# The x of token groups 4 and 5 transposed on TensorE instead of by a DMA transpose

## The chip, the core and the metric

The kernel runs on one core of a Trainium2 chip (trn2). The metric is the device time of one execution in microseconds (us); the kernel before takes 300.17 us, the median of three executions (300.12, 300.17 and 301.02 us). A profiled execution gives the span from the first to the last instruction, 298.4 us, which is a little shorter than the execution's time.

In what follows PE is TensorE (PEld is its loading of weights), DVE is VectorE, ACT is ScalarE, POOL is GpSimd, and SP is SyncE, which computes nothing and here issues nearly all loads and all DMA transposes. A DMA transpose reads a tile from the on-chip memory and writes it back to the on-chip memory transposed, without any compute engine.

## What is computed

Chunked attention, followed by a feed-forward layer with a squared ReLU:

```python
# q, k, v: [8 batches, 8 heads, 576 tokens, 64]; float32
# tokens attend only within their own chunk of 64
scores = (1 / sqrt(64)) * q_c @ k_c.T            # per batch, head and chunk
attn   = softmax(scores)
x      = attn @ v_c                              # then heads side by side:
x      = x.transpose(0, 2, 1, 3).reshape(4608, 512)
h      = maximum(x @ w_in, 0)                    # w_in  [512, 2048]
out    = (h * h) @ w_out                         # w_out [2048, 512]
```

The kernel computes in bfloat16 with float32 sums.

## The kernel before

The 4608 tokens are cut into 18 groups of 256 tokens. Two groups make a block of 512 tokens; there are nine blocks, numbered j = 0 to 8: groups 0 and 1, groups 3 and 2, groups 4 and 5, 6 and 7, and so on. For each block the program runs the first matmul layer (`ffn_in`), then the second (`ffn_out`). The attention of later groups is placed in small steps between these matmuls, at numbered slots: a slot is one `yield` of `ffn_in` or `ffn_out`.

A group goes through these steps: its q and k are cast to bfloat16 (C) and transposed by DMA (TD), or, for the early groups, transposed on TensorE (TA); then scores and exp (SC); then the product with the values and the division (AV), which leaves `x`, tokens on partitions; then `x` is transposed (XT) to `xT`, features on partitions, since `ffn_in` needs it that way.

```python
    blocks = [[0, 1], [3, 2]] + [[g, g + 1] for g in range(4, n_grp, 2)]
    FIRST_DMA_T = 6          # from this group on, q and k are transposed by DMA
    FIRST_DMA_X = 4          # from this group on, x is transposed by DMA
    # ...
    def cast_qk(g):                                               # C, on GpSimd
        qkb = att_pool.tile([128, 2, 2 * H * D], BF16, name="qkb", bufs=2)
        # ... two casts, q and k
    def transpose_qk_dma(g):                                      # TD, issued by SP
        qkT = att_pool.tile([128, 2, 2, n_hp, 128], BF16, name="qkT", bufs=4)
        nc.sync.dma_start_transpose(
            out=qkT.rearrange("c w t h q -> c (w t h) q"),
            in_=qkb.rearrange("p w c -> p (w c)"))
    # ...
    def transpose_x(g):                                           # XT
        j, c = place[g]
        if j not in xTs:
            xTs[j] = att_pool.tile([128, BT // 128, n_dt, 128], BF16, name="xT", bufs=2)
        x = state.pop(("x", g))
        dst = xTs[j][:, c // 128:c // 128 + 2].rearrange("p t h q -> p (t h) q")
        if g >= FIRST_DMA_X:
            nc.sync.dma_start_transpose(out=dst, in_=x.rearrange("p t h a d -> p (t h a d)"))
            return
        ps = ps_att.tile([128, 1024], FP32, name="ps_att")
        psb = ps.bitcast(BF16)[:, 0:1024].rearrange("p (b q) -> p b q", q=128)
        for t in range(2):
            for hp in range(n_hp):
                nc.tensor.transpose(                              # 8 of 128x128, line 337
                    out=psb[:, t * n_hp + hp, :],
                    in_=x[:, t, hp].rearrange("p a d -> p (a d)"),
                    identity=ident)
        copy = nc.scalar.copy if g == 2 else nc.vector.tensor_copy
        copy(out=dst, in_=psb)                                    # line 342
```

The change acts in the plan of block j = 1. That block runs `ffn_in` in 32 slots (0 to 31, four matmuls of 256 columns each) and `ffn_out` in 16 slots (32 to 47, four matmuls of 512 columns each). Its matmuls have groups 3 and 2 for input; between them it prepares the next block (`nxt`: groups 4 and 5) and starts on the one after that (`far`: groups 6 and 7):

```python
        elif j == 1:
            loads = itertools.chain(*map(qk_pieces, far), v_pieces(far[0]))
            go_slots = range(14, 32)          # one load is issued at each of these slots
            # ... group 2: TA, SC, AV, XT at slots 1, 5, 8, 12
            for i, g in enumerate(nxt):       # groups 4 and 5
                for slot, f in ((21 + 4 * i, TA), (28 + 2 * i, SC), (33 + 2 * i, AV),
                                (36 + 2 * i, XT)):
                    at(slot, f, g)
            for i, g in enumerate(far):       # groups 6 and 7
                at(34 + 3 * i, C, g)
                at(39 + 3 * i, TD, g)
```

In block j = 2 the scores of groups 6 and 7 come at slots 8 and 11, their values at 12 and 16, and the transposes of their x at 16 and 19. An `ffn_in` slot there is four matmuls of 512 columns.

Line numbers in the profile that matter here: 123, 130 and 145 are loads (q and k, values of the even heads, values of the odd heads), 272 the DMA transpose of q and k, 286 the scores, 310 the product with the values, 318 the division that writes `x`, 331 the DMA transpose of `x`, 337 and 342 the TensorE transpose of `x` and its copy out of PSUM, 355 the matmuls of `ffn_in`, 402 those of `ffn_out`, and 422 those of the first block's `ffn_out`.

Of the kernel before, what the change touches and what calls it, by code (L numbers as in the profile page):

```python
# [17 lines left out]
def kernel(  # L18
# [21 lines left out]

    blocks = [[0, 1], [3, 2]] + [[g, g + 1] for g in range(4, n_grp, 2)]
    FIRST_DMA_T = 6
    FIRST_DMA_X = 4
    BT = GT * max(len(b) for b in blocks)

    const_pool = ctx.enter_context(tc.tile_pool(name="const", bufs=1))
# [80 lines left out]
    def v_pieces(g):  # L127

        for t, p, m, b, s in runs(g):
            yield lambda t=t, p=p, m=m, b=b, s=s: nc.sync.dma_start(  # L130
                out=v_even[g % NV][p:p + m, t, :, 0:D],
                in_=v[b, 0::2, s:s + m, :].rearrange("h s d -> s h d"))

        g0, g1 = GT * g, GT * (g + 1)
        for n in range(2 * g, 2 * g + 3):
            lo, hi = max(0, 128 * n - 64), min(n_tokens, 128 * n + 64)
            if g in (1, 2, 3):
                lo, hi = max(lo, 320 if g == 1 else g0), min(hi, g1)
            elif g > 3:
                lo = max(lo, g0 if g == 4 else g0 + 64)  # L140
            if lo >= hi:
                continue
            p = lo - (128 * n - 64)
            for b, s, m in segments(lo, hi - lo):
                yield lambda n=n, p=p, m=m, b=b, s=s: nc.sync.dma_start(  # L145
                    out=v_odd[n % NO][p:p + m, :, 0:D],
                    in_=v[b, 1::2, s:s + m, :].rearrange("h s d -> s h d"))
                p += m

    def go(pieces):  # L150
        for f in pieces:
            f()
# [171 lines left out]
    def transpose_x(g):  # L324
# [4 lines left out]
# [3 lines that stand above are left out]
# [12 lines left out]
    C, TD = cast_qk, transpose_qk_dma  # L344
    SC, AV, XT = scores, values, transpose_x
# [24 lines left out]
    def ffn_in(j, parts):  # L370
        for c, n, ft in ((c, n, ft) for c, n, fts in parts for ft in fts):

            o, per = ft * n % 512, 512 // n
            if o == 0:
                h = ps_ffn.tile([128, 512], FP32, name="ps_ffn")
            mm_in(j, h, o, ft, c, n)
            if o + n == 512:
                relu2(j, h, ft + 1 - per, per, c)
            yield

    def ffn_out(j):
        gT = gTs.pop(j)
        n_tt = len(blocks[j]) * GT // 128
        for tt in range(n_tt):
            if j == len(blocks) - 1 and tt == n_tt - 1:

                t0 = blocks[j][tt // 2] * GT + tt % 2 * 128
                for dma, c in ((nc.scalar, 0), (nc.sync, 256)):
                    o_ps = ps_ffn.tile([128, d_model], FP32, name="ps_ffn")
                    for ft in range(n_ft):  # L390
                        nc.tensor.matmul(  # L391
                            out=o_ps[:, 0:256],
                            lhsT=gT[:, ft, tt * 128:(tt + 1) * 128],
                            rhs=w_out_bf[:, ft, c:c + 256],
                            start=(ft == 0), stop=(ft == n_ft - 1))
                    o_sb = ffn_pool.tile([128, d_model], FP32, name="o_sb", bufs=4)
                    nc.vector.tensor_copy(out=o_sb[:, 0:256], in_=o_ps[:, 0:256])
                    dma.dma_start(out=out[t0:t0 + 128, c:c + 256], in_=o_sb[:, 0:256])
                continue
            o_ps = ps_ffn.tile([128, d_model], FP32, name="ps_ffn")  # L400
            for ft in range(n_ft):
                nc.tensor.matmul(  # L402
                    out=o_ps,
                    lhsT=gT[:, ft, tt * 128:(tt + 1) * 128],
                    rhs=w_out_bf[:, ft, :],
                    start=(ft == 0), stop=(ft == n_ft - 1))
                if ft == n_ft - 1:
                    t0 = blocks[j][tt // 2] * GT + tt % 2 * 128
                    o_sb = ffn_pool.tile([128, d_model], FP32, name="o_sb", bufs=4)
                    nc.scalar.copy(out=o_sb, in_=o_ps)  # L410
                    nc.gpsimd.dma_start(out=out[t0:t0 + 128, :], in_=o_sb)  # L411
                if ft % 4 == 3:
                    yield

    def ffn_out_by_ft(j):

        gT = gTs.pop(j)
        n_tt = len(blocks[j]) * GT // 128
        o_ps = [ps_ffn.tile([128, d_model], FP32, name="ps_ffn") for _ in range(n_tt)]

        def mm(tt, ft):
            nc.tensor.matmul(  # L422
                out=o_ps[tt],
                lhsT=gT[:, ft, tt * 128:(tt + 1) * 128],
                rhs=w_out_bf[:, ft, :],
                start=(ft == 0), stop=(ft == n_ft - 1))

        for ft in range(n_ft - 4):
            for tt in range(n_tt):
                mm(tt, ft)  # L430
            yield
        for tt in range(n_tt):
            for ft in range(n_ft - 4, n_ft):
                mm(tt, ft)
            o_sb = ffn_pool.tile([128, d_model], FP32, name="o_sb", bufs=4)
            nc.scalar.copy(out=o_sb, in_=o_ps[tt])
            t0 = blocks[j][tt // 2] * GT + tt % 2 * 128
            nc.gpsimd.dma_start(out=out[t0:t0 + 128, :], in_=o_sb)
            yield

    def pieces(grps):
        for g in grps:
            yield from qk_pieces(g)
        for g in grps:
            yield from v_pieces(g)
# [44 lines left out]
    for j, grps in enumerate(blocks):  # L490
        nxt = blocks[j + 1] if j + 1 < len(blocks) else []
        far = blocks[j + 2] if j + 2 < len(blocks) else []
        plan = {}

        def at(slot, f, g):
            plan.setdefault(slot, []).append((f, g))

        if j == 0:
            loads, go_slots = pieces(far), range(17)
            for slot, f in ((22, TA), (25, SC), (26, AV), (28, XT)):  # L500
                at(slot, f, nxt[0])
            phases = [ffn_in(0, [(0, 512, range(2, n_ft))]), ffn_out_by_ft(0)]
        elif j == 1:
            loads = itertools.chain(*map(qk_pieces, far), v_pieces(far[0]))
            go_slots = range(14, 32)
            for slot, f in ((1, TA), (5, SC), (8, AV), (12, XT)):
                at(slot, f, grps[1])
            for i, g in enumerate(nxt):
                for slot, f in ((21 + 4 * i, TA), (28 + 2 * i, SC), (33 + 2 * i, AV),
                                (36 + 2 * i, XT)):  # L510
                    at(slot, f, g)
            for i, g in enumerate(far):
                at(34 + 3 * i, C, g)
                at(39 + 3 * i, TD, g)
            phases = [ffn_in(1, [(0, 256, range(n_ft)), (256, 256, range(n_ft))]), ffn_out(1)]
        else:
            loads, go_slots = pieces(far), range(32)
            slots = {SC: 9 if j == 3 else 8, AV: 11, XT: 15, C: 14, TD: 19}
            if j == 2:
                loads = itertools.chain(v_pieces(nxt[1]), loads)  # L520
                go_slots = [*range(14), 17, 18, *range(22, 32)]
                slots = {SC: 8, AV: 12, XT: 16, C: 16, TD: 21}
            for i, g in enumerate(nxt):
                at(slots[SC] + (3 * i if j == 2 else 0), SC, g)
                at(slots[AV] + 4 * i, AV, g)
                at(slots[XT] + 3 * i, XT, g)
            for i, g in enumerate(far):
                at(slots[C] + 2 * i, C, g)
                at(slots[TD] + 3 * i, TD, g)
            phases = [ffn_in(j, [(0, BT, range(n_ft))]), ffn_out(j)]  # L530
        slot = 0
        for phase in phases:
            for _ in phase:
                if slot in go_slots:
                    for f in loads:
                        f()
                        break
                for f, g in plan.get(slot, []):
                    f(g)
                slot += 1  # L540
        go(loads)
# [30 lines left out]
```

## Time and profile before

| | |
|---|---|
| time, median of 3 | 300.17 us |
| span of the profiled execution | 298.4 us |
| PE busy | 285.6 us, 96% of the span |
| ACT, DVE, POOL busy | 131.3, 108.2, 65.4 us |
| DMA transposes of x (line 331) | 14, landing 3.0 to 6.2 us after issue, median 3.3 |
| DMA transposes of q and k (line 272) | 12, landing 5.2 to 8.9 us after issue, median 5.7 |
| TensorE transposes of x at line 337 | 16 (groups 3 and 2) |

The profile's page gives busy times, the span in 40 slices with the granted clock of TensorE, the chain of work that ended last, and groups of instructions. For each group it says how long one instruction takes and how long its engine stood idle before it, and for what. Idle time on an engine other than the one that sets the end costs nothing by itself. The timeline shows instructions in order of time; for the queue of SP an entry is the issue of a DMA, not its landing. Where a matmul row gives a mean of 359 to 383 ns, this is the time of one from start to end; matmuls overlap in the pipeline, so the spacing of a row of them is read from the starts in the chain or in the timeline.

### The profile page before, as it was taken

How to read it: one execution, taken by the hardware profiler on the slowest of the kernel's cores; microseconds unless marked ns; L12 is line 12 of the kernel's file. 1: busy time of each engine (PE TensorE's matmuls, PEld its weight loads, DVE VectorE, ACT ScalarE, POOL GpSimd, SP SyncE). 2: the span in 40 equal slices, each digit the busy share in tenths (PEclk: the TensorE clock that was granted, in tenths of full speed). 3: DMA queues.
4: the chain of work that ended last, by engine and by line, in shares of the span. 5: the costliest groups of instructions: out<-in, count | busy, mean ns of one | idle time of the engine just before them, and what ended most of it. 6: DMA issues, size and time to landing. Idle time of an engine off the chain costs nothing.

```text
span 298.4 us, 6449 instructions
## 1 busy us (share of the span) xinstructions
PE 285.6 (96%) x2645; PEld 141.0 (47%) x2645; DVE 108.2 (36%) x232; ACT 131.3 (44%) x214; POOL 65.4 (22%) x103
## 2 busy tenths in 40 slices
PE   6899998999949999999999999999999999999995
PEld 3454445885414444444444444444444444444444
DVE  0467314564103450356037405630662046205401
ACT  1556224775105731672167217712671177126510
POOL 2067634000430241033105014201420100020010
PEclk9999999999997999999999999999999999999999
DMA  7999999997999999999999999699967501310011
GB/s 235 247 348 368 346 268 246 237 206 169 231 232 193 222 182 233 221 213 172 231 227 218 182 265 236 122 175 271 253 120 153 161 36 21 86 73 35 0 73 70
DMA packets 147933, 56.52 MB, mean 189 GB/s; under 512 B 129024, under 2 KB 143616, under 8 KB 147904
## 3 DMA queue, kind: packets, MB, share of 16 engines
q1 hardware_dynamic: 144960, 46.81, 77.1%
q0 software_dynamic: 2800, 9.18, 9.0%
q8 instruction: 21, 0.34, 0.5%
q10 hardware_dynamic: 144, 0.13, 0.1%
q14 instruction: 8, 0.07, 0.1%
HBM read 36.70 MB, written 9.44 MB: 155 GB/s over the span
## 4 chain that ended last, share of the span: by engine, by line
PE 79%; DMA 10%; SPq 7%; POOL 2%; issue 1%; DVE 0%; DVEq 0%
PE ps_ffn L355 38%; PE ps_ffn L402 33%; DMA w_st<-in_moe_w_out_dram 5%; DMA w_st<-in_moe_w_in_dram 4%; SPq L130 3%; PE ps_att L310 2%; SPq L145 2%; DMA xT<-x 2%; PE ps_att L286 2%; SPq L123 1%; PE ps_ffn L391 1%; PE ps_ffn L422 1%; PE ps_att L191 1%; POOL w_out_bf L174 1%; POOL w_in_bf L167 1%
## 5 line engine op out<-in xcount | busy, mean ns | idle before, releaser
L355 PE MATMUL ps_ffn<-xT,w_in_bf 128*128 128x512 bf16 (+3 forms) x648 | 131.5, 359 | 4.0 <-DMA xT<-x 4.0
L367 DVE TENSOR_TENSOR gT<-rl 128x512 bf16<-128x512 bf16 x144 | 69.9, 496 | 147.3 <-ACT rl L365 145.9
L402 PE MATMUL ps_ffn<-w_out_bf,gT 128*128 128x512 bf16 x496 | 108.9, 379 | 0.0
L365 ACT ACTIVATE rl<-ps_ffn 128x512 bf16<-128x512 f32 x144 | 85.1, 599 | 42.4 <-PE ps_ffn L355 41.0
L355 PEld LDWEIGHTS <-w_in_bf 128*128 128x128 bf16 x648 | 61.6, 98 | 65.2 <-issue 6.6
L402 PEld LDWEIGHTS <-gT 128*128 128x128 bf16 x496 | 47.9, 98 | 56.8
L410 ACT COPY o_sb<-ps_ffn 128x512 f32<-128x512 f32 x31 | 18.2, 586 | 92.3 <-PE ps_ffn L402 92.3
L411 POOL DMA_DIRECT2D out_dram<-o_sb x31 | 16.8, 541 | 124.2 <-ACT o_sb L410 124.2
L265 POOL CAST qkb<-qk_sb 128x1024 bf16<-128x1024 f32 x24 | 26.7, 1125 | 74.1 <-DMA qk_sb<-in_q_dram 72.2
L318 DVE TENSOR_TENSOR x<-ps_att,rec 128x512 bf16<-128x512 f32 x36 | 24.9, 691 | 1.2
L293 ACT ACTIVATE e<-ps_att 128x1024 bf16<-128x1024 f32 x18 | 17.7, 1023 | 2.3 <-PE ps_att L286 2.3
L422 PE MATMUL ps_ffn<-w_out_bf,gT 128*128 128x512 bf16 x64 | 15.0, 379 | 1.4 <-POOL w_out_bf L174 1.3
L174 POOL CAST w_out_bf<-w_st 128x1024 bf16<-128x1024 f32 x8 | 8.7, 1086 | 8.2 <-DMA w_st<-in_moe_w_out_dram 7.9
L259 PE MATMUL ps_ffn<-zeros 128*128 128x512 bf16 x29 | 8.9, 439 | 1.3 <-POOL zeros L58 1.3
L317 DVE RECIPROCAL rec<-ps_att 128x8 f32<-128x8 f32 x36 | 7.2, 199 | 8.2 <-PE ps_att L310 8.1
L310 PEld LDWEIGHTS <-e 64*64 64x64 bf16 x576 | 6.5, 107 | 7.5 <-issue 3.2
L422 PEld LDWEIGHTS <-gT 128*128 128x128 bf16 x64 | 6.0, 98 | 8.5 <-issue 1.6
L310 PE MATMUL ps_att<-ve_sb,e 64*64 64x65 bf16 x288 | 8.8, 196 | 0.1
L310 PE MATMUL ps_att<-vo_sb,e 64*64 64x65 bf16 x288 | 8.7, 196 | 0.0
L200 ACT COPY qkT<-ps_att 128x512 bf16<-128x512 bf16 x8 | 4.3, 589 | 9.9 <-PE ps_att L191 9.9
L167 POOL CAST w_in_bf<-w_st 128x1024 bf16<-128x1024 f32 x7 | 7.6, 1086 | 2.9 <-DMA w_st<-in_moe_w_in_dram 2.9
L286 PEld LDWEIGHTS <-qkT 64*64 64x64 bf16 x576 | 5.7, 108 | 4.7 <-issue 3.0
(34 smaller groups left out, 58.5 us busy)
## 6 DMA issues: line engine op xcount, KB each, us to landing
out_dram<-o_sb POOLq DMA_DIRECT2D x35, 256.0 KB, 4.2
qk_sb<-in_q_dram SPq DMA_DIRECT2D x23, 256.0 KB, 5.5
qk_sb<-in_k_dram SPq DMA_DIRECT2D x23, 256.0 KB, 5.6
ve_sb<-in_v_dram SPq DMA_DIRECT2D x32, 128.0 KB, 4.4
w_st<-in_moe_w_in_dram SPq DMA_DIRECT2D x8, 512.0 KB, 6.6
w_st<-in_moe_w_out_dram SPq DMA_DIRECT2D x8, 512.0 KB, 6.5
vo_sb<-in_v_dram SPq DMA_DIRECT2D x29, 128.0 KB, 3.8
qk_sb<-in_q_dram SPq DMA_DIRECT2D x1, 1024.0 KB, 5.7
```

What stands on the lines that cost most here:

```text
L174: nc.gpsimd.tensor_copy(out=w_out_bf[:, 2 * i:2 * i + 2, :], in_=st)
L265: nc.gpsimd.tensor_copy(out=qkb[:, which], in_=qk[g][which].rearrange("p t h d -> p (t h d)"))
L293: nc.scalar.activation(out=e.rearrange("p a h t q -> p (a h t q)"), in_=ps, func=AF.Exp, scale=scale)
L310: nc.tensor.matmul(out=ps[64 * p:64 * p + 64, a, hp * (D + 1):(hp + 1) * (D + 1)], lhsT=e[64 * c:64 * c + 64, a, hp, t, :], rhs=vb[64 * c: ...
L318: nc.vector.tensor_tensor(out=x[:, t].rearrange("p h a d -> p a h d"), in0=o[:, :, :, 0:D], in1=rec.to_broadcast([128, 2, n_hp, D]), op=AL ...
L355: nc.tensor.matmul(out=h[:, o:o + n], lhsT=w_in_bf[:, dt, ft * 128:(ft + 1) * 128], rhs=xT[:, c // 128:(c + n) // 128, dt, :], start=(dt = ...
L365: nc.scalar.activation(out=rl, in_=h, func=AF.Relu)
L367: nc.vector.tensor_tensor(out=gTs[j][:, ft:ft + per, c:c + 512 // per], in0=r3, in1=r3, op=ALU.mult)
L402: nc.tensor.matmul(out=o_ps, lhsT=gT[:, ft, tt * 128:(tt + 1) * 128], rhs=w_out_bf[:, ft, :], start=(ft == 0), stop=(ft == n_ft - 1))
L410: nc.scalar.copy(out=o_sb, in_=o_ps)
L411: nc.gpsimd.dma_start(out=out[t0:t0 + 128, :], in_=o_sb)
L422: nc.tensor.matmul(out=o_ps[tt], lhsT=gT[:, ft, tt * 128:(tt + 1) * 128], rhs=w_out_bf[:, ft, :], start=(ft == 0), stop=(ft == n_ft - 1))
```

## The change

The x of groups 4 and 5 is no longer transposed by two DMA transposes. It takes the way that groups 2 and 3 already take: eight TensorE transposes per group into PSUM, and one copy to `xT`, which is on VectorE for groups 4 and 5. The transposes are placed at slots 38 and 41 instead of 36 and 38. The DMA transposes of q and k of groups 6 and 7 move up three slots, from 39 and 42 to 36 and 39. The change is meant to spare the next block's first matmul the wait for a transfer, and SP's queue two entries.

```diff
-    FIRST_DMA_X = 4
+    FIRST_DMA_X = 6
...
                 for slot, f in ((21 + 4 * i, TA), (28 + 2 * i, SC), (33 + 2 * i, AV),
-                                (36 + 2 * i, XT)):
+                                (38 + 3 * i, XT)):
                     at(slot, f, g)
             for i, g in enumerate(far):
                 at(34 + 3 * i, C, g)
-                at(39 + 3 * i, TD, g)
+                at(36 + 3 * i, TD, g)
```

On the engines this adds 16 transposes to PE (eight after the 28th of the 64 matmuls of block 1's `ffn_out`, eight after the 40th) and two copies to DVE, and takes two DMA transposes from SP's queue. ACT and POOL have the same instructions in the same order.

## The prediction

> **What bounds the kernel now.** I read four views, in this order. First the page's totals and slices: TensorE is busy 96% of the span, so the other engines set the end only where TensorE waits for them.
>
> ```profile
> PE 285.6 (96%) x2645; PEld 141.0 (47%) x2645; DVE 108.2 (36%) x232; ACT 131.3 (44%) x214; POOL 65.4 (22%) x103
> ...
> PEclk9999999999997999999999999999999999999999
> ```
>
> The clock row has one dent, a 7 in the thirteenth slice. A slice is 298.4 / 40 = 7.46 us, so the dent lies between 89.5 and 97.0 us. Next, the groups: among the many matmuls of the two layers only line 355 has a wait worth naming.
>
> ```profile
> L355 PE MATMUL ps_ffn<-xT,w_in_bf 128*128 128x512 bf16 (+3 forms) x648 | 131.5, 359 | 4.0 <-DMA xT<-x 4.0
> L402 PE MATMUL ps_ffn<-w_out_bf,gT 128*128 128x512 bf16 x496 | 108.9, 379 | 0.0
> ```
>
> The end of the first row says that TensorE stood idle for 4.0 us, and that a DMA writing xT ended it. The table of waits says once, not 14 times. So one of the transposes of x comes late, and the others are hidden. The chain in order of time shows which one; the columns are start, length, what:
>
> ```profile
> 73.85 0.59 PE ps_att L310 x32
> 74.44 0.26 SPq L123
> ...
> 81.94 1.34 SPq L331
> ...
> 83.39 5.17 DMA xT<-x
> 88.56 0.14 issue
> 88.69 9.62 PE ps_ffn L355 x36
> 98.31 0.38 PE ps_att L286 x32
> ```
>
> It is the transpose of group 5, at the start of block 2. At 74.44 us the chain leaves TensorE for SP's queue. The timeline says why: x of groups 4 and 5 was written by 73.73 and 75.95 us, but SP issues in order, and before the two transposes it still had loads to issue, without a pause, until 81.83 us. The transposes went out at 81.94 and 83.39 us, the second took 5.17 us to land, and TensorE had run out of ffn_out's matmuls: 48 of them from 74.17 us at 217.5 ns (the spacing in block 2, 13.92 us for 64) end at 84.61 us.
>
> Last, the stretches. Columns: stretch, length, busy time of PE, PEld, DVE, ACT and POOL, granted clock, DMA share, GB/s.
>
> ```profile
> 84.70:88.70 4.00, 0.01 (x2) 0.04 (x2) 0.00 (x0) 0.59 (x1) 0.54 (x1) 1.00 1.12 275
> ...
> 89.50:92.90 3.40, 3.40 (x10) 1.22 (x8) 0.85 (x2) 1.20 (x2) 0.00 (x0) 0.50 1.43 169
> 92.90:98.30 5.40, 5.40 (x31) 2.31 (x33) 2.31 (x6) 3.58 (x6) 0.00 (x0) 1.00 0.96 214
> ```
>
> TensorE is idle for 4.0 us, and soon after it resumes its clock is halved for 3.4 us. "Busy 3.40" hides this: ten matmuls began there, where 3.40 / 0.216 = 15.7 would fit. The wait is thus paid for twice. The same stretch of the next block, also 36 matmuls between the start and the first scores, needs 7.77 us instead of 9.62:
>
> ```profile
> 149.68 7.77 PE ps_ffn L355 x36
> ```
>
> **What the Trainium skill says.** "TensorE: Matmul & The Clock Gate", section "Why this matters for your kernels", advises no idle gaps of TensorE over about 3 us, since the clock then falls to half; Part 1 there gives the activity window as 3413 ns and says that it runs freely. The trace agrees: 4.0 us idle, then 3.4 us at 0.50. Part 4 of the same page says that a TensorE transpose needs a copy out of PSUM afterwards, and that transposes don't count as activity in the same way; here eight last 0.45 to 0.60 us, and no dent follows those at 48 and 58 us. "VectorE: DVE Perf Modes", section "The three transpose paths", gives 390 ns for a TensorE transpose of 128x128 and 1309 ns for a DMA one. I use neither: in a row the trace spaces TensorE's far closer, and this DMA's cost is its place in the queue.
>
> **The change, part by part.**
>
> 1. *Removed: the wait.* TensorE would go on at 84.61 instead of 88.69 us: 4.08 us gained, all on the path.
> 2. *Removed: the half clock.* Without the pause I expect no throttle: 9.62 - 7.77 = 1.85 us gained, also on the path.
> 3. *Added on TensorE: 16 transposes.* The same instruction runs for groups 3 and 2 already:
>
> ```profile
> 48.40 0.45 PE ps_att L337 x8
> ...
> 57.80 0.60 PE ps_att L337 x8
> ```
>
> Two groups cost 2 x 0.45 = 0.90 to 2 x 0.60 = 1.20 us. They lie between matmuls of ffn_out and TensorE has no slack there, so all of it counts. I take the middle, 1.05 us.
> 4. *Added on VectorE: two copies of 128x1024.* One takes 0.69 us (line 342, group 3). From the last division at 75.95 us to 90.44 us VectorE does nothing, so both are hidden. Are they in time? Group 4's transposes start after 28 matmuls of ffn_out, at 74.17 + 12 x 0.2175 = 76.8 us, when both x are complete. Group 5's start 12 matmuls later, at 79.8 us; with the copy, xT is there by about 81.3 us. ffn_out now ends at 84.61 + 1.05 = 85.7 us, so over 4 us are left. The PSUM tiles of ps_att were last read by the division at 75.95 us and are free.
> 5. *Removed from SP: two issues, 2.8 us in all.* The transposes of q and k of groups 6 and 7 then follow the loads directly, at about 81.9 instead of 84.9 us. Nothing waits for them now (before, they land at 93.8 and 95.4 us; the scores start at 98.24 and 101.31), so no gain. But the question is whether they still land in time.
>
> Sum: 4.08 + 1.85 - 1.05 = **4.9 us**, from 300.17 to **295.3 us**, 1.6%.
>
> **Rivals.**
>
> *A: the next transposes become the wait.* TensorE reaches the scores of group 6 at 85.7 + 7.8 = 93.5 us, and those of group 7 after 12 more matmuls and the first scores, at about 96.5 us: each some 4.8 us sooner, while SP moves by only some 3 us. The first transpose, issued at 81.94 us, lands by 90.8 us even with the slowest landing on record (8.9 us): 2.7 us to spare. The second is issued after it, at 86.8 us if the first holds the queue for 4.8 us again, and lands at 92.3 us with 5.5 us, or 95.7 with 8.9: 0.8 us to spare at worst. Against the rival: the slow landing stood behind the two transposes that now go away. If it comes true, the gain falls by a microsecond or so, unless the pause grows long enough to halve the clock again.
>
> *B: SP's backlog shows a block later.* The last transpose of x for block 4 lands at 146.25 us and is needed at 149.68, a margin of 3.4 us. If TensorE moves by 4.9 us and SP by 2.8, the margin shrinks by 2.1 to 1.3 us. The transposes for block 3 land at 113.19 us for a start at 120.31: more room. From 188 us on SP pauses for x by itself, so the backlog is gone. I expect no wait, but one of up to 1 us is possible.
>
> *C: the transfer was hidden anyway, and the transposes only cost time:* about 301.2 us. This would be so had TensorE another reason to stand still at 84.6 us. Against it: the chain passes through this transfer, and other blocks start without a pause after their ffn_out. I give it almost nothing.
>
> *D: the wait goes, the half clock stays* (because transposes don't count as activity): 297.2 us. Against it: transposes fill only about 1 us of the 85.7 us before, and equal rows of them at 48 and 58 us left no dent.
>
> **Range and chances.** The sum with the cheapest transposes gives 295.1 us, with the dearest 295.4. I expect no reward in later blocks, since after 88.69 us TensorE has no pause that could shrink; the most that can be gained is 4.08 + 1.85 = 5.9 us, to 294.2, if the transposes cost nothing. On the slow side A and B can return a microsecond or so, and D 1.85. The medians wander by some tenths (one execution of three was 0.85 us above the others). So 295.3, range 294.6 to 296.9. A gain of over 2% needs a time below 294.17, beyond that largest gain: chance 0.03. Slower by over 2% would need a new pause of over 10 us: 0.01.
>
> **What would show it right or wrong.** Right: no wait of line 355 for xT; no dent in the clock row between 89 and 97 us; line 337 with 32 transposes, a row of eight taking 0.45 to 0.60 us; 36 matmuls in 7.8 us from about 85.7 us; then the same lengths as before in every later block. Step 3 is wrong if the two rows cost other than 0.9 to 1.2 us, seen as ffn_out of block 1 growing by another amount. Rival A would show as a wait of line 286 for qkT near 93 or 96 us, B as a wait of line 355 for xT near 145 us, D as a halved clock with no pause ahead of it.

## The result, and the profile after

The changed kernel takes **295.63 us** (median of four executions, 295.15 to 296.68) against 300.14 us before on the same chip: a ratio of 0.985, with a 95% interval of 0.9815 to 0.9886. The gain is 4.5 us; 4.9 was predicted.

From the page of the changed kernel, the same rows as those shown of before: totals, clock in 40 slices, the two layers' matmuls.

```profile
PE 285.2 (97%) x2661; PEld 141.7 (48%) x2661; DVE 111.1 (38%) x234; ACT 131.2 (45%) x214; POOL 64.7 (22%) x103
...
PEclk9999999999999999999999999999999999999999
...
L355 PE MATMUL ps_ffn<-xT,w_in_bf 128*128 128x512 bf16 (+3 forms) x648 | 129.8, 356 | 0.0
...
L402 PE MATMUL ps_ffn<-w_out_bf,gT 128*128 128x512 bf16 x496 | 109.3, 379 | 0.0
```

The wait of 4.0 us at the end of the row of line 355 is 0.0, and the dent in the clock is gone. The 16 added transposes show only in the counts (2645 to 2661): "busy" of TensorE is even 0.4 us lower, since matmuls at half clock count as busy for longer (line 355 falls from 131.5 to 129.8 us), and the idle time had never counted. The chain that ended last, around the end of block 1 (start, length, what):

```profile
74.87 2.70 PE ps_ffn L402 x12
77.57 0.45 PE ps_att L337 x8
78.02 2.59 PE ps_ffn L402 x12
80.61 0.45 PE ps_att L337 x8
81.05 5.18 PE ps_ffn L402 x24
86.23 7.77 PE ps_ffn L355 x36
94.00 0.38 PE ps_att L286 x32
```

The chain stays on TensorE. Before, it left for SP's queue at 74.44 us and came back at 88.69. The two rows of transposes take 0.45 us each, block 2 starts at once after ffn_out, and its first 36 matmuls take 7.77 us instead of 9.62.

In the span (298.4 to 294.1 us) the gain is 4.3 us. The balance: block 1's ffn_out starts 0.64 us later than before (70.53 against 69.89 us). In this execution TensorE stood still for 0.88 us at 55.6 us, inside line 310, and the profile names no releaser for it. From there to block 3 (69.89 to 120.31 us before, 70.53 to 116.01 after) the gain is 4.94 us.

### The profile page after: what moved, and what is told of

It reads as the page before. It is cut to its first block, busy times and chain, and to the rows that moved or that the text cites. A ratio compares the mean times of both kernels' runs of the same rounds, so it can differ in the third digit from the quotient of the medians.

```text
span 294.1 us, 6475 instructions
## 1 busy us (share of the span) xinstructions
PE 285.2 (97%) x2661; PEld 141.7 (48%) x2661; DVE 111.1 (38%) x234; ACT 131.2 (45%) x214; POOL 64.7 (22%) x103
## 4 chain that ended last, share of the span: by engine, by line
PE 83%; DMA 9%; SPq 4%; POOL 2%; issue 1%; DVE 0%; DVEq 0%
PE ps_ffn L355 38%; PE ps_ffn L402 37%; DMA w_st<-in_moe_w_out_dram 5%; DMA w_st<-in_moe_w_in_dram 4%; PE ps_att L310 2%; SPq L130 2%; PE ps_att L286 2%; SPq L145 2%; PE ps_ffn L391 1%; PE ps_ffn L422 1%; PE ps_att L191 1%; POOL w_out_bf L174 1%; POOL w_in_bf L167 1%; PE ps_att L337 1%; POOL w_in_bf L163 1%
## 5 line engine op out<-in xcount | busy, mean ns | idle before, releaser
L355 PE MATMUL ps_ffn<-xT,w_in_bf 128*128 128x512 bf16 (+3 forms) x648 | 129.8, 356 | 0.0
L367 DVE TENSOR_TENSOR gT<-rl 128x512 bf16<-128x512 bf16 x144 | 71.3, 508 | 136.3 <-ACT rl L365 135.0
L265 POOL CAST qkb<-qk_sb 128x1024 bf16<-128x1024 f32 x24 | 26.0, 1105 | 69.0 <-DMA qk_sb<-in_q_dram 67.8
L259 PE MATMUL ps_ffn<-zeros 128*128 128x512 bf16 x29 | 9.5, 464 | 1.3 <-POOL zeros L58 1.3
```

Source lines behind the costliest of these rows:

```text
L265: nc.gpsimd.tensor_copy(out=qkb[:, which], in_=qk[g][which].rearrange("p t h d -> p (t h d)"))
L355: nc.tensor.matmul(out=h[:, o:o + n], lhsT=w_in_bf[:, dt, ft * 128:(ft + 1) * 128], rhs=xT[:, c // 128:(c + n) // 128, dt, :], start=(dt = ...
L367: nc.vector.tensor_tensor(out=gTs[j][:, ft:ft + per, c:c + 512 // per], in0=r3, in1=r3, op=ALU.mult)
```

## The experiments

**1. The moves without TensorE.** The changed plan, x still by DMA:

```diff
-    FIRST_DMA_X = 6
+    FIRST_DMA_X = 4
```

> The changed plan with the transposes of x of groups 4 and 5 left to the DMA: on SP's queue they now come in the order q and k of 6, x of 4, q and k of 7, x of 5. Theory (the gain is the wait for xT taken away; the moves bring nothing by themselves): x of group 5 is issued some 6 us later than in the kernel before, at about 88 to 90 us, lands at about 93 us, the pause grows to about 8 us with the half clock after it, and the time is about 304.5 us. Rival (the gain comes from the earlier transposes of q and k): at or below 300 us.

Measured: 304.92 us, ratio to the kernel before 1.0199 (1.0127 to 1.0271). Its chain, and its row among the waits (us in total, times, longest):

```profile
88.72 3.49 DMA xT<-x
...
92.35 10.06 PE ps_ffn L355 x36
```

```profile
PE ps_ffn L355 <- DMA xT<-x: 7.8, 1, 7.8
```

The pause grows from 4.0 to 7.8 us, since both transposes of q and k now stand ahead of group 5's x, which goes out at 88.72 instead of 83.39 us. The moves alone are a loss; the same order of slots becomes harmless only once x no longer goes through SP's queue.

**2. TensorE without the moves.** The kernel before with `FIRST_DMA_X = 6`, nothing else.

> The kernel before with x of groups 4 and 5 transposed on TensorE, and no slot moved. Theory: SP's queue has the same entries in the same order as in the changed kernel, since the two DMA transposes of x were all that stood between; TensorE's transposes come 8 and 12 matmuls earlier and nothing waits for them: same time as the changed kernel, 295.6 us within 0.5. Rival (the moves matter): 1 us or more above the changed kernel, with a wait of the scores of block 2 or of the copies from PSUM.

Measured: 295.14 us, ratio 0.9879 (0.9832 to 0.9926), no wait for xT. That is the changed kernel's time within what can be told apart. With experiment 1 this settles it: to within about half a microsecond, the whole gain comes from the one constant.

**3. The changed kernel again,** on two other chips.

> The changed kernel unaltered, on the same chip as the others of this call: 295.5 us. The idle time of 0.9 us inside the values of group 2 near 56 us, which its first profile shows without a releaser, should be gone if it was chance, and there again if the change causes it.

> The changed kernel unaltered, as the measure for the others of this call: 295.3 us, no wait for xT, a whole clock.

Measured: 295.31 us, ratio 0.9881 (0.9831 to 0.9932), and 295.22 us, ratio 0.9901 (0.9869 to 0.9932). One of the 12 executions behind the second median took 300.32 us at a mean clock of 0.994; it has no trace, so what it waited for stays open.

The idle time at 55.6 us is in neither profile (spans 293.1 and 292.9 us). Both kernels of experiment 8, with x on the DMA, stand still at the same place: for 0.54 us until 56.75 us, without a named releaser, and for 0.69 us until 56.14 us, where the profile names a load of group 2's values. So it comes and goes with or without the change; its cause stayed open.

That the ratios are nearer to 1 here lies with the kernel before: its medians on these two chips were 299.43 and 299.05 us instead of 300.14, so that the medians differ by 4.1 and 3.8 us. The ratios leave out every execution more than 1.5% above the fastest of its kernel; on the three chips where the kernel before ran often (those of experiments 1, 4 and 9) these are 33 of its 105 executions, all with a mean clock of 0.994 or less, which brings the ratios nearer to 1 still.

**4. A pause without a late transfer.** To the changed kernel, one step is added at slot 47, the last of block 1: VectorE multiplies zeros 24 times, and a matmul waits for the result.

```diff
+    scr = const_pool.tile([128, 512], BF16, name="scr")
+
+    def pause(n):
+        for _ in range(n):
+            nc.vector.tensor_tensor(out=scr, in0=zeros, in1=zeros, op=ALU.mult)
+        ps = ps_ffn.tile([128, 512], FP32, name="ps_ffn")
+        nc.tensor.matmul(out=ps, lhsT=zeros[:, 0:128], rhs=scr, start=True, stop=True)
...
+            at(47, pause, 24)
```

> The changed kernel with a pause of TensorE made without any late transfer: 24 multiplications of 128x512 zeros on VectorE (about 0.43 us each) after its copies for group 5, and one matmul before block 2 that reads their result. VectorE starts them at about 81.5 us and ends near 91.8, so TensorE stands idle for some 5.5 to 6 us. Theory (idle time of TensorE by itself halves the clock afterwards): the clock drops to 0.50 for 3.4 or 6.8 us, the next 36 matmuls take 9.5 to 10.6 us instead of 7.8, and the time is 295.5 + 5.8 + 1.7 to 2.8 = 303 to 304 us. Rival (the half clock comes from the DMA traffic, or only with late DMA transposes): whole clock, 36 matmuls in 7.8 us, about 301.3 us.

Measured: 305.04 us, ratio 1.0217 (1.0141 to 1.0294). In the timeline the dummy matmul (line 453 of this kernel) waits for VectorE; then two stretches (columns as before: length, busy times, clock, DMA share, GB/s):

```profile
92.27 0.61 PE L453 MATMUL ps_ffn<-scr,zeros 128*128 128x512 bf16 x1 [7.37 <-DVE scr L451]
```

```profile
88.60:95.40 6.80, 3.13 (x8) 1.20 (x9) 3.52 (x9) 0.60 (x1) 0.00 (x0) 0.50 1.25 242
95.40:101.90 6.50, 6.50 (x31) 2.74 (x28) 3.78 (x8) 4.18 (x7) 2.89 (x3) 1.00 1.35 217
```

Nothing is late here, xT was ready, and still the clock is at 0.50 for 6.8 us around the end of the pause. Nor is it the traffic: in the changed kernel without a pause (experiment 3, second profile) the DMAs moved as much at the same time, and the clock was whole. The second half of the pause, and the same stretch there:

```profile
88.60:92.27 3.67, 0.00 (x0) 0.00 (x1) 3.37 (x8) 0.00 (x0) 0.00 (x0) 0.50 1.16 262
```

```profile
88.60:92.30 3.70, 3.70 (x19) 1.70 (x18) 1.84 (x5) 2.64 (x5) 0.00 (x0) 1.00 1.14 260
```

So it is TensorE's own idleness that halves the clock, not the traffic or the late transposes. The pause was longer than planned: the multiplications took 11.85 us together instead of 10.3. Twenty-two of them lasted 0.43 us, as I had counted, but began 0.46 us apart, and the first two took 1.69 us. That accounts for the time above the expected 303 to 304.

**5. The pause filled.** The kernel before with matmuls on zeros between the two layers, 14 of them and then 7:

```diff
+            at(47, keep_busy, 14)
```

> The kernel before, with 14 matmuls on zeros (128x512, nothing uses their result) put between block 1's last matmul of ffn_out and block 2's first of ffn_in, so that TensorE works through most of the pause while the DMA transpose of group 5 is still late. Theory: the late transfer ends the wait at the same moment (88.7 us), but the pause shrinks to about 1 us, the clock stays whole, and the first 36 matmuls of block 2 take 7.8 us instead of 9.6: about 298.3 us, 1.85 below the kernel before. Rival (the half clock has another cause than the pause, such as the traffic of the DMAs then): the clock still falls to 0.50, and the time stays at 300.2.

> The kernel before with 7 instead of 14 matmuls on zeros in the pause. With 14 the clock stayed whole in most executions but the time fell by only 0.6 us. Theory (the 14 also held TensorE up in the executions in which the transfer landed before they were through at 87.6 us): 7 are through at 86.1 us, hold it up less often, and still leave under 3 us of the pause: the clock stays whole in most executions and the time falls by 1 to 1.8 us. Rival (a whole clock there is not worth 1.85 us): again 0.6 us or less with a whole clock.

Measured: 298.66 us with 14, ratio 0.9986 (0.996 to 1.0013); 297.71 us with 7, ratio 0.9994 (0.9965 to 1.0023). By the ratios neither gain can be told from nothing, so neither expectation is borne out. The clock did respond. With 14, 16 of 20 executions kept a mean clock of 0.997 or more, of the kernel before on that chip 5 of 23; with 7, 18 of 22, against 14 of 39. The medians of all executions fell by 0.6 us (from 299.25) and by 1.3 us (from 299.05). How much a whole clock is worth here was thus not settled.

In part the expectation was at fault: it took the pause of 4.0 us and the 300.2 us for those of every execution. The time expected with 14, 298.3 us, was nearly met; it was the kernel before that came in lower. The two profiles, both of executions slower than the median (303.71 and 301.17 us), show a pause of another length in each, first with 14 and then with 7:

```profile
84.13 7.08 DMA xT<-x
...
91.35 10.55 PE ps_ffn L355 x36
```

```profile
83.41 6.38 DMA xT<-x
...
89.92 9.37 PE ps_ffn L355 x36
```

In the kernel before, the same transfer took 5.17 us. Here it came so late that after the matmuls on zeros, which ended at 87.18 and 86.27 us, TensorE still stood idle for 4.16 and 3.65 us, and the clock was halved all the same. Where the transfer comes sooner, the 14 matmuls hold TensorE up; no such execution was traced.

**6. Three times the transposes.** The changed kernel with each transpose of groups 4 and 5 done three times:

```diff
-        for t in range(2):
+        for t in list(range(2)) * (3 if g in (4, 5) else 1):
```

> The changed kernel with every TensorE transpose of groups 4 and 5 done three times over into the same place in PSUM (the copy follows the last): 32 transposes more. If a row of eight costs 0.45 us on the path and nothing else, as in the profile of the changed kernel, the rows become 1.35 us each and the time 295.5 + 4 x 0.45 = 297.3 us, with a whole clock. If long rows of transposes count as idle for the clock (rival D of the prediction), or stall on PSUM, more than that, with a dent in the clock.

Measured: 297.19 us, ratio 0.9934 (0.9912 to 0.9956). From its chain:

```profile
77.61 1.34 PE ps_att L337 x24
81.54 1.34 PE ps_att L337 x24
...
88.06 7.77 PE ps_ffn L355 x36
```

A row of 24 takes 1.34 us, three times 0.45. The time is 1.9 us above the changed kernel on the same chip (295.31); 4 x 0.45 = 1.8 was expected. The cost of a transpose on the path is thus 56 ns, and after 1.34 us of nothing but transposes the clock is whole. This does not show that transposes count as activity: 1.66 us of true idleness left the clock whole as well (experiment 8, first version).

**7. The transfer made earlier, by order.** The kernel before, the five loads of group 6's values moved behind all four transposes on SP's queue:

```diff
-            go_slots = range(14, 32)
+            go_slots = [*range(14, 24), *range(43, 48)]
...
-                at(39 + 3 * i, TD, g)
+                at(40 + 2 * i, TD, g)
```

> The kernel before, with both transposes of x still on the DMA, but with the values of group 6 (five loads) moved behind all four transposes on SP's queue, so that x of groups 4 and 5 goes out at about 78.1 and 79.5 us and lands by 84.7, when TensorE needs it. It adds nothing on TensorE. If the wait at block 2 is all there is, the time is 300.1 - 4.1 - 1.85 = 294.2 us, 1 to 1.5 us better than the changed kernel. If SP's backlog matters (it keeps the 2.8 us of issues that the changed kernel drops, while TensorE arrives 5.9 us sooner), new waits come up in blocks 2 to 4: some 0.7 us for q and k of group 9 and up to 2.4 us for x of group 9 at the start of block 4; then 295.5 to 297.5 us.

Measured: 295.99 us (293.77 to 296.5), ratio 0.9888 (0.983 to 0.9946). The first pause is gone: x of group 5 lands at 83.05 us and block 2 starts at 84.12. But among TensorE's waits two are new:

```profile
PE ps_att L286 <- DMA qkT<-qkb: 1.4, 1, 1.4
...
PE ps_ffn L355 <- DMA xT<-x: 0.3, 1, 0.3
```

The first is at 153.3 us, for group 11's q and k in block 4; the second at 114.2 us, for x at the start of block 3. The expectation had named transfers of group 9, but the sum of 1.7 us and the time lie in its second range. In part this is rival B: SP kept its 2.8 us of issues, so that the two transfers went out only 1.5 and 2.6 us sooner than in the kernel before (at 144.35 and 107.23 us), while TensorE came some 6 us sooner. But they also took longer to land, 8.95 us instead of 6.75 and 6.93 instead of 3.35. With the landings of the kernel before they would have been there at 151.1 and 110.6 us, ahead of TensorE at 151.9 and 113.9. One profile does not say whether the longer landings belong to this order or to this execution. That the change is also of use by relieving SP is therefore likely, but not shown.

**8. The transfer made earlier, by another queue.** The kernel before with the same five loads issued by GpSimd, first in their old place in the program and then behind the casts of groups 6 and 7:

```diff
 # v_pieces also takes the issuing engine (not shown)
-            loads = itertools.chain(*map(qk_pieces, far), v_pieces(far[0]))
+            loads = itertools.chain(*map(qk_pieces, far), v_pieces(far[0], nc.gpsimd))
 # second version also:
-            go_slots = range(14, 32)
+            go_slots = [*range(14, 24), *range(38, 43)]
```

> The kernel before with x still transposed by DMA and all slots as they were, but with the five loads of group 6's values issued by GpSimd instead of SP. It relieves SP by 3.8 us of issues and costs no engine's time on the path. Theory (SP's order and backlog made the transfer late): the two transposes of x go out at about 78.1 and 79.5 us and land by 83 to 84.7 us; no pause, no half clock, and unlike the version that only reordered SP's queue no new waits in blocks 3 and 4: 294.0 to 294.6 us, about 1 us below the changed kernel. Rival (the loads from GpSimd are slower or crowd out the transposes): the pause comes back in part, or the values of group 6 come late near 98 us, and the time is 296 us or more.

> The kernel before, x by DMA, with group 6's values loaded from GpSimd's queue again, but placed in GpSimd's order behind the casts of groups 6 and 7 (at about 83 us), so that they can no longer crowd the loads of group 5 and do not stand ahead of the transposes of x. No work is added to TensorE. Theory (order, not bandwidth, made the transfer late): the transposes of x go out at about 78.1 and 79.5 us, land by 84.7, there is no pause and the clock is whole; the values land near 90 us, before their use at 97: about 294.4 us, 0.9 below the changed kernel. Rival (with x by DMA something later always comes due, as in the two other versions that kept it): a wait in blocks 2 to 4 of 1 us or more, and the time is that of the changed kernel, 295.3 us, or above.

Measured: the first 296.76 us, ratio 0.9948 (0.9923 to 0.9973); the second 295.54 us (293.8 to 296.44), ratio 0.9845 (0.9812 to 0.9878). Waits of the first, in the profile of its slowest execution (299.15 us):

```profile
PE ps_ffn L355 <- DMA xT<-x: 1.8, 2, 1.7
PE ps_att L191 <- DMA qk_sb<-in_k_dram: 1.4, 2, 1.0
```

GpSimd had nothing else to do and issued the five loads at 51.7 us, some 26 us before SP did in the kernel before. They then shared the DMA engines with the q and k of groups 4 and 5, of which the last landed 13.3 us after issue, at 68.33 us instead of 64.77. SP's whole queue slipped with it: x of group 4 went out at 81.69 us, not at 78.1. Behind the casts the loads do no harm: the transposes of x go out at 77.68 and 80.36 us and land by 83.68, with no wait for them and a whole clock: the expected mechanism. The expected time of 294.4 us was missed, though: this version is no better than the changed kernel, within what its six executions can tell, and the 0.9 us of transposes that it saves I could not show in the time.

**9. Half and half.** The changed kernel with group 4's x by DMA, ahead of group 6's values on SP's queue, and only group 5's on TensorE:

```diff
-        if g >= FIRST_DMA_X:
+        if g >= FIRST_DMA_X and g != 5:          # FIRST_DMA_X = 4
...
-            go_slots = range(14, 32)             # x of 4 and 5 at slots 36 and 41,
+            go_slots = [*range(14, 24), *range(43, 48)]   # q and k of 6, 7 at 37, 40
```

> The changed kernel with group 4's x back on the DMA, placed on SP's queue ahead of the values of group 6, and only group 5's x on TensorE. It should spare one row of eight transposes, 0.45 us. Theory: the transfer of group 4 goes out at about 77 us and lands by 83, before TensorE needs it; SP has 1.4 us of issues more than in the changed kernel, and the margins there (4.7 to 7 us for the later transposes) bear that: 294.9 us, 0.45 below the changed kernel of the same call, a whole clock. Rival (SP's backlog costs again, as when both transposes were only moved ahead): a wait for q and k of block 3 or 4 eats the gain, and it equals the changed kernel or is slower.

Measured: 295.47 us (294.5 to 297.29), ratio 0.992 (0.9885 to 0.9956), beside 295.22 us of the changed kernel on the same chip. Block 2 starts at 84.64 us in its profile and at 85.05 in the other, so the 0.4 us are there on the path, and no wait took their place; but the medians don't show them. No version tried is clearly better than the changed kernel.

## Why the prediction was right

1. *The wait is gone:* confirmed. It was the only wait of line 355 for xT, and it was there because of what SP had to issue first. Experiments 7 and 8 (second version) remove it by making the transfer earlier, with x still on the DMA; experiment 1 makes it longer by putting two more entries ahead.
2. *The half clock is gone:* confirmed in the profile, 9.62 to 7.77 us, and its cause shown by experiment 4. Of the 22 executions of the changed kernel, 21 had a mean clock of 0.998 or more; the other is the one of 300.32 us in experiment 3.
3. *16 transposes for 0.90 to 1.20 us:* 0.90, the lower end; experiment 6 measured it by tripling. I had taken 1.05.
4. *The copies are hidden and in time:* the second one ran from 81.09 to 81.78 us, 4.4 us before block 2 began; "over 4 us left" was right.
5. *SP and the next transposes:* in time, but the size was off. The transposes for groups 6 and 7 landed at 88.68 and 91.22 us for scores at 94.00 and 97.08: over 5 us to spare, where rival A reckoned with 2.7 and 0.8 at worst. For rival B I let SP move by 2.8 us and the margin at block 4 shrink to 1.3. It was 4.7 us: the transpose landed at 140.68 instead of 146.25, 5.6 us sooner for a start at 145.38: issued 3.8 us sooner (136.26 instead of 140.07), and landed in 4.42 us instead of 6.18. The term that was mis-sized is "SP moves by 2.8 us", the two issues that it loses. The transposes of q and k that followed also held SP for a shorter time (6.87 us for the two instead of 8.35) and began 3.6 us sooner. SP went on to the next loads at 88.26 us instead of 93.37.

C and D did not happen, as the first and second point show; D's reason, that transposes don't count as activity, was not tested. B did not come up in the changed kernel. Experiment 7 has waits of its kind in a neighbouring version, but only together with longer landings.

The mechanism and the sum held in the two traces: the stretch from block 1's ffn_out to block 3 gained 4.94 us. That the medians came so close too, with 4.5 us, was in part luck, since the sum stood on one execution of the kernel before and its pause is not a constant. On the two other chips the medians differ by 4.1 and 3.8 us. The 105 executions of the kernel before on the three chips named in experiment 3 fall into three groups:

| mean clock | executions | median, us | above 295.3 us |
|---|---|---|---|
| 0.997 or more | 24 | 297.06 | 1.8 |
| 0.992 to 0.994 | 60 | 299.39 | 4.1 |
| 0.987 to 0.989 | 21 | 301.24 | 5.9 |

The profile of the kernel before, with 3.4 us at half clock, has a mean of 0.993; the profiles with 6.8 us (experiments 1 and 4, and 5 with 14 matmuls) have 0.987 to 0.989. So the change is worth least where the pause was too short to halve the clock, and most where it was halved for longest. This is read from the clocks, for these executions have no trace. What can vary is seen in the three that have one: with the same order on SP's queue, x of group 5 took 5.17, 6.38 and 7.08 us to land. The prediction's range allowed for a spread of the medians of tenths; it had no term for the pause to differ from one execution to the next.

## What to carry to other kernels

Where a transfer ends the only wait of a busy TensorE, look at what stands ahead of it in its queue before looking at how long it takes: here x was ready at 75.95 us, and SP came to it at 83.39. Count a pause of TensorE of some 4 us as 5 to 7, and as a quantity that varies between executions: pauses of 3.65, 3.99 and 4.16 us, with the slow matmuls behind them, cost 5.2, 5.8 and 6.9 us. Work that TensorE does in 0.45 us can be cheaper than a transfer that costs it nothing, if the queue is late; and moving loads to an idle engine's queue may start them too early.

## What was not expected of the hardware

The half-clock stretches came in two lengths. One profile each, in us from the start of the span, lengths in brackets:

| profile | TensorE idle | clock at half |
|---|---|---|
| experiment 8, first version | 87.51 to 89.17 (1.66) | not at all |
| experiment 5, 7 matmuls | 86.27 to 89.92 (3.65) | 89.45 to 92.86 (3.41) |
| the kernel before | 84.71 to 88.69 (3.99) | 89.53 to 92.95 (3.41) |
| experiment 5, 14 matmuls | 87.18 to 91.35 (4.16) | 89.86 to 96.68 (6.83) |
| experiment 4 | 84.90 to 92.27 (7.37) | 88.62 to 95.45 (6.83) |
| experiment 1 | 84.55 to 92.35 (7.80) | 89.84 to 96.67 (6.83) |

The half clock can begin while TensorE still waits, or after it has gone on. Its length does not grow evenly with the pause: 3.99 us led to 3.4, and 4.16 us to 6.8. What decides between the two was not tested. A transpose took 56 ns in a row of 24.
